# A fused attention and feed-forward kernel: a new order of steps from the eighth batch's kv sums on

## The chip, the cores and the metric

The kernel runs on one core of a Trainium2 chip. A core has five engines, each with its own queue of instructions that it takes strictly in order: PE (TensorE, matrix products), DVE (VectorE), ACT (ScalarE), POOL (GpSimd) and SP (SyncE, which here issues nearly all DMAs). Semaphores tie the queues together. The metric is the device time of one execution in microseconds (us); lower is better.

## The reference

It is an attention with cosine weights, whose output is the input of a two-layer feed-forward net.

```python
# q, k, v: (8, 8, 576, 64); c, s: cos and sin of pi/2 * position/576
def phi(x, c, s):
    r = np.maximum(x, 0.0)
    return np.concatenate([r * c, r * s], axis=-1)
q_p, k_p = phi(q, cos_w, sin_w), phi(k, cos_w, sin_w)
kv = np.einsum('bhsf,bhsd->bhfd', k_p, v)
z = np.sum(k_p, axis=2)
num = np.einsum('bhsf,bhfd->bhsd', q_p, kv)
den = np.einsum('bhsf,bhf->bhs', q_p, z)[..., None] + 1e-06
x = (num / den).transpose(0, 2, 1, 3).reshape(4608, 512)
...
h = x @ w_in                    # 512 x 2048
g = np.maximum(0.01 * h, h)
return g @ w_out                # 2048 x 512
```

## The kernel before

**The work.** There are nine groups of 512 tokens: groups 0 to 7 are the first 512 tokens of each batch, and group 8 collects the last 64 tokens of all eight batches. For a batch b, `k_cos(b,j,e)` and `k_sin(b,j,e)` make the weighted keys of token block j (tile kp, L428 on DVE and POOL, L426 on ACT), `v_pairs` casts the values (tile vm), and `kv_sum(b,...)` is the sum over tokens of keys times values: 72 small matmuls on PE (L503) and a cast by ACT to the tile kv (L510). `q_prep(g,j,...)` weights the queries (tile qp), `q_transpose_dma` turns them by DMA (tile qpT), `num(g,j)` multiplies them by kv on PE (L587), `den` and `rec` take the denominators, and `mul` writes x (tile xs). `x_transpose_dma(g)` turns that into the tile xT. `load_qtail(i)` loads the queries of two batches' tails for group 8 (tile qtl; two DMAs, L311) into a buffer that result tiles use as well: both have the tag osb, with four buffers.

**The feed-forward.** Each of the two large products is cut in halves of both operands and done with seven products of half the size in place of eight (the known scheme of Strassen, in a form with shared sums). `P(g,u,n)` is product n of the first layer for unit u of group g: four matmuls of 128x128 by 128x256 (L791). `x_sum(g,n,e)` makes the sums of xT's pieces that some of these products take. `e(g,u,x)` are the steps that read them out: b, s and S are copies (b on ACT, B on DVE; s on ACT, S on DVE), w and y are adds on DVE (L684), and a, c, d and e are the leaky relu on ACT, which write the tiles G. `g_sum` are sums of G's pieces on DVE. `F(g,i)` are products of the second layer, four matmuls each (L910), `R(g,n,e)` read their results out to the tiles osb, and `S(g,n)` stores a result (one DMA on SP, L1117).

For group 7, the eighth batch, each half-size product of the second layer is cut once more. Its operands' sums are the 28 steps `TS(n,k,e)` (`t_sum`, four sums of w_out's pieces for each of the products 1 to 7, tile tsum, 128x512 numbers in f16) and `AS(g,n,k,e)` (`a_sum`, the same for G's pieces, tile asum). `F2(g,n,j)` are the products (L1058), `R2` reads out, `C` combines. A helper, `tt_op`, records every sum of two tensors, so these all stand as L684.

**The order.** Nothing is scheduled when the kernel runs. A table PROGRAM lists all 1455 steps in the order in which they are recorded; each engine's queue is what is left of that list for it, and tiles and semaphores follow from it. The last letter of most steps names the engine: D for DVE, A for ACT, P for POOL. So a step that moves in the table may move on one engine, past what stands ahead of it there, and a changed letter takes the work to another queue.

```python
for name, args in parse(PROGRAM):
    OPS[name](*args)
```

The kv sums of the eighth batch, `kv_sum(7,0,4,n)`, stand in the table behind most of group 5's first layer and some of group 6's.

Of the kernel before, what the change touches and what calls it, by code (L numbers as in the profile page):

```python
# [107 lines left out]
e(5,1,e) k_sin(7,1,A) R(4,2,A) F(4,12) e(5,2,b) P(5,1,4) S(3,5) P(5,2,6) num(6,3) P(5,2,2) g_sum(4,3,5,8,2)  # L108
k_sin(7,0,D) e(5,1,d) e(5,2,a) e(5,1,c) e(5,2,w) q_prep(7,1,0,8,P) F(4,13) k_sin(7,5,P) den(6,3) load(v,7) S(3,3)
S(3,4) q_transpose_dma(7,0) F(4,14) P(5,2,3) P(5,3,1) F(4,15) P(5,2,7) P(5,3,5) F(4,16) rec(6,3) g_sum(4,4,0,4)  # L110
mul(6,3) e(5,2,e) e(5,2,y) e(5,3,b) x_transpose_dma(6) e(5,3,s) v_pairs(7,2,4,A) e(5,2,c) F(4,17) P(5,3,6) P(5,3,2)
k_cos(7,2,D) load_qtail(0) R(4,7,D) g_sum(4,4,4,8) e(5,3,w) F(4,20) F(4,18) P(5,2,4) F(4,21) F(4,19) R(4,5,D) P(5,3,7)
e(5,3,y) k_cos(7,0,D) q_prep(7,3,0,8,D) x_sum(6,1,D) k_cos(7,4,A) e(5,3,a) P(5,3,3) F(4,22) e(5,2,d) e(5,3,c)
x_sum(6,3,D) F(4,24) F(4,25) F(4,23) P(6,0,1) F(4,26) F(4,27) P(5,3,4) g_sum(5,1,4,8,2) x_sum(6,2,D) k_sin(7,8,P)
v_pairs(7,0,2,P) TS(1,1,P) k_sin(7,6,P) TS(6,1,P) k_cos(7,3,P) k_sin(7,7,P) e(5,3,e) e(6,0,b) P(6,0,5) e(5,3,d)
P(6,0,2) k_cos(7,1,D) P(6,0,6) P(6,1,1) e(6,0,a) e(6,0,s) k_cos(7,5,D) k_cos(7,6,D) k_sin(7,2,A) R(4,4,D) k_cos(7,7,D)
# [5 lines left out]
F(5,8) P(6,2,1) q_prep(8,2,0,8,P) den(7,1) q_prep(8,1,0,8,A) e(6,1,y) rec(7,1) mul(7,1) num(7,2) F(5,9) P(6,1,4)
e(6,1,e) R(5,6,D) TS(1,4,D) TS(5,1,D) e(6,2,s) e(6,2,b) e(6,1,d) TS(2,4,D) TS(1,3,D) S(4,3) S(4,2) load_qtail(3)
q_transpose_dma(8,0) P(6,2,6) F(5,10) P(6,3,1) F(5,11) e(6,2,w) R(5,2,A) den(7,2) P(6,2,3) F(5,12) F(5,16) num(7,3)
P(6,2,2) e(6,2,e) e(6,2,a) e(6,3,b) e(6,1,c) q_prep(8,3,0,8,A) g_sum(5,3,5,8,2) rec(7,2) TS(7,1,D) mul(7,2) den(7,3)
rec(7,3) F(5,13) P(6,2,7) P(6,3,5) F(5,14) P(6,3,2) F(5,15) F(5,17) num(8,0) P(6,3,6) F(5,18) mul(7,3) F(5,19)
R(5,7,D) e(6,2,y) e(6,3,s) e(6,2,c) e(6,3,a) TS(4,3,P) TS(6,2,P) TS(5,2,P) g_sum(5,4,4,8) g_sum(5,4,0,4)
x_transpose_dma(7) den(8,0) e(6,3,w) R(5,5,D) F(5,20) F(5,21) F(5,22) F(5,23) P(6,3,7) P(6,2,4) x_sum(7,1,P) TS(7,3,P)
e(6,3,y) R(5,4,D) P(6,3,3) F(5,24) x_sum(7,3,D) g_sum(6,1,0,4,1) g_sum(6,1,4,8,2) TS(4,1,D) e(6,2,d) e(6,3,c) P(6,3,4)
F(6,0) F(5,25) P(7,0,1) x_sum(7,2,D) e(6,3,e) e(6,3,d) e(7,0,b) g_sum(6,2,4,8,2) rec(8,0) mul(8,0) P(7,0,5) F(5,26)  # L130
P(7,0,6) F(6,1) g_sum(6,1,5,8,2) F(6,2) F(5,27) num(8,1) P(7,0,2) e(7,0,s) e(7,0,a) TS(6,4,D) e(7,0,w) F(6,3) P(7,0,3)
R(6,1,A) e(7,0,e) g_sum(6,2,0,4,1) R(5,3,D) den(8,1) x_sum(7,4,D) g_sum(6,2,5,8,2) P(7,0,7) F(6,4) P(7,1,1) P(7,1,5)
e(7,1,b) g_sum(6,3,5,8,2) e(7,0,y) g_sum(6,3,4,8,2) rec(8,1) e(7,1,S) e(7,0,c) q_transpose_dma(8,1) F(6,8) F(6,5)
F(6,6) P(7,1,6) F(6,9) num(8,2) F(6,7) mul(8,1) e(7,1,w) den(8,2) F(6,10) P(7,1,7) rec(8,2) TS(4,2,D) mul(8,2)
g_sum(6,3,0,4,1) R(6,6,D) P(7,0,4) P(7,1,2) F(6,11) P(7,1,3) F(6,12) num(8,3) e(7,1,y) e(7,1,a) TS(2,3,D)
g_sum(6,4,0,4) den(8,3) TS(7,2,D) TS(5,3,D) rec(8,3) mul(8,3) e(7,0,d) S(5,4) S(5,2) F(6,13) P(7,2,1) P(7,2,5)
R(6,2,A) e(7,1,e) e(7,2,b) e(7,2,s) e(7,1,c) P(7,1,4) F(6,16) P(7,2,6) F(6,17) F(6,14) P(7,2,2) TS(7,4,P) TS(5,4,P)
TS(6,3,D) x_transpose_dma(8) e(7,2,w) e(7,1,d) e(7,2,a) P(7,2,7) P(7,2,3) P(7,3,1) F(6,18) F(6,15) P(7,3,5) e(7,2,e)
g_sum(6,4,4,8) e(7,2,y) TS(4,4,D) TS(3,1,D) e(7,3,b) x_sum(8,1,P) e(7,2,c) e(7,3,s) P(7,3,6) g_sum(7,1,0,4,1) F(6,19)
P(7,2,4) e(7,3,w) R(6,7,D) P(7,3,2) e(7,2,d) x_sum(8,2,P) P(7,3,7) P(8,0,1) F(6,20) P(7,3,3) e(7,3,y) g_sum(7,3,0,4,1)  # L140
TS(3,3,D) S(5,3) S(5,5) g_sum(7,2,0,4,1) P(7,3,4) F(6,21) e(7,3,c) e(7,3,e) R(6,5,D) e(7,3,a) e(8,0,b) e(7,3,d)
F(6,22) F(6,23) P(8,0,5) AS(7,2,1,D) F2(7,1,1) x_sum(8,4,P) AS(7,1,1,D) AS(7,1,2,P) P(8,0,6) P(8,0,2) F2(7,1,2)
F(6,24) F(6,25) F(6,26) e(8,0,s) F2(7,1,4) R(6,4,D) x_sum(8,3,D) g_sum(7,1,4,8,2) AS(7,2,2,D) e(8,0,w) AS(7,1,3,D)
AS(7,2,3,D) AS(7,1,4,D) F(6,27) F2(7,1,5) P(8,0,7) F2(7,1,6) R(6,3,D) e(8,0,y) P(8,0,3) F2(7,1,7) g_sum(7,3,4,8,2)
F2(7,1,3) P(8,1,1) g_sum(7,1,5,8,2) AS(7,2,4,D) g_sum(7,2,4,8,2) TS(3,2,D) g_sum(7,2,5,8,2) TS(3,4,D) AS(7,6,1,D)
AS(7,5,1,D) e(8,0,a) R2(7,1,A) P(8,1,5) F2(7,6,1) AS(7,6,3,D) AS(7,6,2,D) S(6,5) S(6,2) S(6,3) P(8,0,4) F2(7,2,1)
F2(7,2,2) F2(7,2,4) AS(7,6,4,D) e(8,1,s) e(8,0,e) e(8,1,b) F2(7,2,5) F2(7,2,6) F2(7,2,7) F2(7,2,3) P(8,1,2) F2(7,6,2)
P(8,1,6) R2(7,2,A) C(7,2,1,P) e(8,1,w) e(8,1,a) e(8,0,c) F2(7,6,4) F2(7,6,5) g_sum(7,3,5,8,2) F2(7,6,7) F2(7,5,1)
F2(7,5,2) F2(7,6,6) F2(7,5,4) P(8,2,5) F2(7,6,3) P(8,1,3) P(8,1,7) C(7,2,2,D) AS(7,5,3,D) AS(7,7,1,D) g_sum(7,4,0,4)
e(8,1,y) e(8,0,d) R2(7,6,A) AS(7,5,2,P) AS(7,7,2,P) F2(7,7,1) P(8,2,1) F2(7,5,5) F2(7,7,2) e(8,1,e) e(8,2,b) e(8,2,S)  # L150
AS(7,7,3,D) AS(7,5,4,D) AS(7,7,4,D) e(8,1,c) F2(7,7,4) F2(7,7,5) P(8,2,2) F2(7,5,6) F2(7,7,6) P(8,1,4) F2(7,5,7)
g_sum(7,4,4,8) F2(7,5,3) F2(7,7,7) F2(7,7,3) P(8,2,6) AS(7,4,1,D) e(8,2,a) e(8,1,d) R2(7,7,A) AS(7,3,1,D) e(8,2,w)
AS(7,4,2,P) R2(7,5,D) C(7,5,1,P) C(7,5,2,P) AS(7,4,4,P) C(7,5,4,P) P(8,3,5) F2(7,4,1) F2(7,4,2) AS(7,4,3,D) F2(7,4,5)
P(8,2,7) P(8,2,3) P(8,3,1) F2(7,3,1) F2(7,4,4) F2(7,3,2) e(8,2,y) e(8,2,e) e(8,3,b) P(8,2,4) P(8,3,6) F2(7,3,4)
F2(7,4,7) F2(7,3,5) AS(7,3,3,D) AS(7,3,2,D) F2(7,3,6) F2(7,4,6) F2(7,3,7) F2(7,4,3) e(8,3,s) e(8,2,c) R2(7,4,A)
e(8,2,d) e(8,3,w) P(8,3,7) AS(7,3,4,D) g_sum(8,1,0,4,1) P(8,3,3) F2(7,3,3) P(8,3,2) e(8,3,y) P(8,3,4) e(8,3,e)
e(8,3,a) e(8,3,c) e(8,3,d) g_sum(8,1,4,8,2) R2(7,3,D) C(7,4,1,P) C(7,2,4,P) g_sum(8,1,5,8,2) g_sum(8,2,0,4,1)
g_sum(8,2,4,8,2) g_sum(8,3,4,8,2) g_sum(8,2,5,8,2) C(7,5,3,D) C(7,3,1,D) F(8,0) F(8,20) F(8,16) F(8,1) F(8,2) F(8,4)
F(8,3) R(8,1,A) F(8,5) F(8,6) F(8,8) F(8,7) F(8,9) C(7,2,3,P) C(7,4,2,D) g_sum(8,3,5,8,2) C(7,4,3,D) g_sum(8,3,0,4,1)
C(7,3,2,D) R(8,6,D) F(8,10) F(8,11) F(8,17) R(8,2,A) F(8,12) F(8,13) C(7,3,4,D) g_sum(8,4,0,8) C(7,3,3,D) F(8,14)  # L160
C(7,4,4,P) F(8,15) F(8,21) F(8,18) F(8,19) F(8,22) F(8,23) R(8,7,D) R(8,5,D,0) R(8,4,D) R(8,5,D,1) F(8,24) S(6,4)
# [1196 lines left out]
```

## Time and profile before

| | |
|---|---|
| Median of 3 runs | 271.87 us (271.45 to 272.15) |
| Profiled execution | 271.46 us |
| Its span, first to last instruction | 269.7 us |
| Mean granted PE clock | 0.997 |
| Instructions in the span | 7414 |
| DMA | 57.09 MB in 75041 packets |

The span is what the trace shows; 1.76 us of the execution lie around it. In the page an engine's line gives its busy time, the share of the span and the number of instructions. In a timeline a row is: start, length, engine, line, operation, output <- inputs, shape, and in brackets how long the engine had been idle and what ended that. Rows that follow each other alike are put in one, with their count after an x. The profile names tiles by name without a buffer's number. "SPq" is SP issuing a DMA; the DMA's own time from issue to landing is given apart.

### The profile page before, as it was taken

What the parts mean: (1) busy time and instruction counts of PE and PEld (TensorE: products, weight loads), DVE (VectorE), ACT (ScalarE), POOL (GpSimd) and SP (SyncE); (2) the same over time, 40 slices, a digit from 0 to 9 for tenths busy, and PEclk for the clock granted to TensorE, in tenths of its full rate; (3) what the DMA queues carried; (4) which work ended last, traced back from release to release, by engine and by line L of the source; (5) the groups of instructions that cost most, each with busy time, mean ns of one, the idle gap of its engine ahead of it and who ended that gap; (6) DMA issues with size and microseconds to landing.
All of it is one profiled execution on the core that took longest, in us unless ns stands there. A gap on an engine that the chain in (4) does not pass through costs nothing.

```text
span 269.7 us, 7414 instructions
## 1 busy us (share of the span) xinstructions
PE 261.9 (97%) x3009; PEld 222.9 (83%) x3009; DVE 225.1 (83%) x485; ACT 184.8 (69%) x333; POOL 111.3 (41%) x99
## 2 busy tenths in 40 slices
...
GB/s 232 359 396 413 379 400 371 389 243 238 255 242 337 116 237 231 324 238 259 233 265 191 155 393 147 156 157 121 117 158 79 2 79 79 106 52 2 41 115 158
DMA packets 75041, 57.09 MB, mean 212 GB/s; under 512 B 47232, under 2 KB 63616, under 8 KB 74624
## 3 DMA queue, kind: packets, MB, share of 16 engines
...
q14 instruction: 10, 0.08, 0.1%
...
## 4 chain that ended last, share of the span: by engine, by line
PE 86%; ACT 5%; DMA 3%; DVE 3%; issue 1%; SPq 1%; ACTq 0%; DVEq 0%
PE ps_f L791 31%; PE ps L910 26%; PE ps_h L634 10%; PE ps_o L658 5%; PE ps_kv L503 3%; DMA vst<-in_v_dram 3%; PE ps_num L587 2%; PE ps L1058 2%; ACT qp L426 2%; PE ps_y L1058 2%; PE ps_f L910 1%; ACT vm L434 1%; PE ps_xT L1207 1%; ACT G L823 1%; PE ps_kv L1158 1%
## 5 line engine op out<-in xcount | busy, mean ns | idle before, releaser
L823 ACT ACTIVATE G<-ps_f 128x512 f16<-128x512 f32 x84 | 48.7, 597 | 29.2 <-PE ps_f L791 26.4
L910 PE MATMUL ps<-w,G 128*128 128x256 f16 x432 | 59.6, 273 | 0.1
L910 PEld LDWEIGHTS <-G 128*128 128x128 f16 x560 | 53.7, 98 | 5.9 <-DVE G L684 0.4
L791 PE MATMUL ps_f<-xT,w 128*128 128x256 f16 x336 | 49.4, 273 | 0.1
L791 PEld LDWEIGHTS <-w 128*128 128x128 f16 x448 | 47.8, 113 | 1.1 <-issue 0.2
L791 PEld LDWEIGHTS <-wsum 128*128 128x128 f16 x336 | 36.2, 114 | 2.3 <-issue 1.0
L910 PE MATMUL ps<-T,ext 128*128 128x256 f16 x208 | 29.6, 273 | 0.0
L634 PE MATMUL ps_h<-xT,w 128*128 128x512 f16 (+1 forms) x144 | 29.1, 355 | 0.0
L428 POOL TENSOR_SCALAR kp<-kst,sin_t 128x256 f16<-128x256 f32 x17 | 22.7, 1341 | 11.2 <-PE ps_kv L503 6.2
L791 PE MATMUL ps_f<-X,wsum 128*128 128x256 f16 x176 | 26.0, 273 | 0.3 <-ACT s L434 0.3
L634 PEld LDWEIGHTS <-w 128*128 128x128 f16 x144 | 15.9, 114 | 10.9 <-POOL w L436 0.2
L910 PEld LDWEIGHTS <-ext 128*128 128x128 f16 x224 | 21.6, 98 | 2.2
L684 DVE TENSOR_TENSOR ps_f<-ps_f,s 128x512 f32<-128x512 f32 x28 | 19.4, 694 | 4.5 <-PE ps_f L791 2.4
L684 DVE TENSOR_TENSOR y<-ps_f,s 128x512 f32<-128x512 f32 x28 | 19.2, 684 | 3.6 <-PE ps_f L791 2.6
L645 ACT ACTIVATE G<-ps_h 128x1024 f16<-128x1024 f32 x16 | 15.9, 1022 | 7.2 <-PE ps_h L634 7.2
L611 DVE TENSOR_TENSOR xs<-ps_num,rden 128x512 f16<-128x512 f32 x28 | 19.3, 688 | 0.7
L823 ACT ACTIVATE G<-y 128x512 f16<-128x512 f32 x28 | 17.7, 632 | 2.6 <-DVE y L684 2.5
L428 POOL TENSOR_SCALAR qp<-qst,cos_t 128x512 f16<-128x512 f32 (+1 forms) x5 | 9.5, 1907 | 22.1 <-DMA qpT<-qp 17.8
L434 ACT COPY ps_f<-ps_f 128x512 f32<-128x512 f32 x27 | 15.6, 578 | 3.5 <-PE ps_f L791 3.1
L791 PE MATMUL ps_f<-xT,wsum 128*128 128x256 f16 x112 | 16.8, 273 | 0.8 <-DVE ps_f L684 0.8
L791 PE MATMUL ps_f<-X,w 128*128 128x256 f16 x112 | 16.8, 273 | 0.0
L684 DVE TENSOR_TENSOR osb<-ps,ext 128x512 f32<-128x512 f32 x20 | 13.6, 684 | 3.0 <-PE ps L910 2.8
...
## 6 DMA issues: line engine op xcount, KB each, us to landing
...
```

Source lines behind the costliest of these rows:

```text
L428: eng.tensor_scalar(out=o, in0=i, scalar1=0.0, scalar2=col, op0=ALU.max, op1=ALU.mult)
L434: nc.scalar.copy(o, i)
L503: nc.tensor.matmul(ps[:, o, (c - lo) * NE : (c - lo + 1) * NE], lhsT=st["kp", b][sl, c, j, :], rhs=vm[sl, c, j, :], start=(j == 0), stop=( ...
L611: nc.vector.tensor_tensor(out=xs(), in0=ps[:, :, 0 : 4 * NE].rearrange("p a (b e) -> p a b e", e=NE)[:, :, :, 0:D], in1=st["rden", *k].rea ...
L634: nc.tensor.matmul(ps[:, m % 2, lo:hi], lhsT=w1[m // 4, c][0][:, w1[m // 4, c][1], m % 4 : 512 : 4], rhs=xT[:, lo // P : hi // P, c, :], s ...
L645: nc.scalar.activation(st["g", g][:, m - 1 : m + 1, :], ps, AF.Lrelu)
L658: nc.tensor.matmul(st["ps_o", g, tt], lhsT=st["g", g][:, m, tt * P : (tt + 1) * P], rhs=w2[:, m, :], start=(m == 0), stop=(m == NFT - 1),)
L684: eng.tensor_tensor(out=o, in0=a, in1=b, op=op)
L791: nc.tensor.matmul(ps[:, mi * HT : (mi + 1) * HT], lhsT=a[:, c, 2 * r0 + mi : 512 : 4], rhs=b[:, c], start=(n in (1, 5) and mi == 0 and c ...
L823: nc.scalar.activation(st["g", g][:, m : m + 2, r * HT : (r + 1) * HT], {"a": A, "c": y22, "e": E, "d": B_}[e].rearrange("p (m t) -> p m t ...
L910: nc.tensor.matmul(ps[:, tt], lhsT=a[:, i, tt * P : (tt + 1) * P], rhs=b[:, i], start=(first and i == 4 * halves[0]), stop=(i == NPR - 1 a ...
L1058: nc.tensor.matmul(ps, lhsT=a[:, i], rhs=b[:, i], start=(fresh and i == 0), stop=(i == NI - 1), skip_group_check=True,)
```

## The change

The table PROGRAM gets a new order from its 833rd step to its end, and 39 steps another engine. The steps themselves are the same 1455, with the same sizes. In words: the steps ahead of the eighth batch's kv sums are placed as they would be if group 7 had no second cut, the kv sums themselves stand earlier among the products, and the sums TS, which the table had put partly in front of the kv sums, stand behind it, all but `TS(1,1,P)` and `TS(1,3,P)`; the steps behind have new places. The table has one line fewer, so line numbers of the functions are lower by one (L684 becomes L683).

```diff
-P(6,0,3) q_prep(8,0,0,8,A) F(5,3) e(6,0,e) e(6,1,b) kv_sum(7,0,4,n) S(4,5) g_sum(5,2,5,8,2) e(6,0,y)
...
+x_sum(6,3,D) R(4,4,D) e(6,0,s) e(6,0,w) R(4,3,D) g_sum(5,1,4,8,2) load_qtail(0) q_prep(8,0,0,8,A) kv_sum(7,0,4,n)
...
```

Steps that change the engine: `k_sin(7,1)`, `(7,3)` and `k_cos(7,4)` go from ACT to DVE, `k_sin(7,0)` and `k_cos(7,2)` from DVE to POOL, `q_prep(7,3)` and `k_cos(7,1)`, `(7,5)`, `(7,6)` and `(7,7)` from DVE to ACT, `k_sin(7,2)` and `q_prep(8,1)` from ACT to POOL, `q_prep(8,2)`, `k_sin(7,5)` and `(7,7)` from POOL to ACT, `e(5,3,s)` from ACT to DVE; `x_sum(6,4)`, `(7,2)` and `(8,3)` from DVE to POOL and `(8,1)`, `(8,2)`, `(8,4)` from POOL to DVE; of the sums TS five go from POOL to DVE and five the other way; three AS and four C change as well.

On DVE, from the sum g_sum(4,3,5,8,2) on (the first row; before, the second row is k_sin(7,0), and the add into ps_f is e(5,2,w)):

```order
L684 TENSOR_TENSOR G0_95<-G0_95 128x2x256
L428 TENSOR_SCALAR kp_2842<-kst_2838,sin_t_160 128x4x64
L684 TENSOR_TENSOR ps_f1_1378<-ps_f2_1379,s5_183 128x512
L597 TENSOR_SCALAR den_2907<-ps_num_2881 128x8
L603 RECIPROCAL rden_2944<-den_2907 128x8
```

And now:

```order
L683 TENSOR_TENSOR G0_95<-G0_95 128x2x256
L683 TENSOR_TENSOR ps_f1_1378<-ps_f2_1379,s5_183 128x512
L427 TENSOR_SCALAR kp_2842<-kst_2838,sin_t_160 128x4x64
L596 TENSOR_SCALAR den_2911<-ps_num_2897 128x8
L602 RECIPROCAL rden_2952<-den_2911 128x8
```

The add e(5,2,w) now follows the sum directly; the kp row behind it is k_sin(7,3), and k_sin(7,0) is on POOL.

On POOL beside it, from q_prep(7,1) (the two qp rows) to the last of the eighth batch's keys that POOL makes (vm is the cast v_pairs, tsum are sums of w_out's pieces), before:

```order
L428 TENSOR_SCALAR qp_2789<-qst_2420,cos_t_159 128x8x64
L428 TENSOR_SCALAR qp_2789<-qst_2420,sin_t_160 128x8x64
L428 TENSOR_SCALAR kp_2842<-kst_2838,sin_t_160 128x4x64 x2
L436 CAST vm_167<-vst_2909 128x18x64
L684 TENSOR_TENSOR tsum_3051<-w2_105 128x512
L428 TENSOR_SCALAR kp_2842<-kst_2838,sin_t_160 128x4x64
L684 TENSOR_TENSOR tsum_3054<-T2_178 128x512
L428 TENSOR_SCALAR kp_2842<-kst_2838,cos_t_159 128x4x64
L428 TENSOR_SCALAR kp_2842<-kst_2838,sin_t_160 128x4x64
```

And now, up to q_prep(8,1):

```order
L427 TENSOR_SCALAR qp_2789<-qst_2420,cos_t_159 128x8x64
L427 TENSOR_SCALAR qp_2789<-qst_2420,sin_t_160 128x8x64
L427 TENSOR_SCALAR kp_2842<-kst_2838,sin_t_160 128x4x64
L683 TENSOR_TENSOR tsum_2914<-w2_105 128x512
L427 TENSOR_SCALAR kp_2842<-kst_2838,sin_t_160 128x4x64
L427 TENSOR_SCALAR kp_2842<-kst_2838,cos_t_159 128x4x64
L435 CAST vm_167<-vst_2906 128x18x64
L683 TENSOR_TENSOR tsum_2914<-w2_105 128x512
L427 TENSOR_SCALAR kp_2842<-kst_2838,sin_t_160 128x4x64 x2
L427 TENSOR_SCALAR kp_2842<-kst_2838,cos_t_159 128x4x64
L427 TENSOR_SCALAR qp_3096<-qtl_2945,cos_t_159 128x8x64
L427 TENSOR_SCALAR qp_3096<-qtl_2945,sin_t_160 128x8x64
```

The cast moved behind one sum and two more key steps, and a pair of query steps on a tail tile stands behind the keys.

On SP, from the queries' transpose of group 7 (q_transpose_dma(7,0)) on, before:

```order
L540 DMA_TRANSPOSE qpT_2913<-qp_2789 128x16x128
L554 DMA_TRANSPOSE xT_2951<-xs_2766 128x16x128
L311 DMA qtl_2969<-in_q_dram 64x8x64 x2
L1117 DMA out_0_dram<-osb_2995 128x2x256
L540 DMA_TRANSPOSE qpT_3203<-qp_2773 128x16x128
L311 DMA qtl_3205<-in_q_dram 64x8x64 x2
```

And now (the first pair of tail loads is load_qtail(1), osb_2999 is S(4,5), and the second pair is load_qtail(0)):

```order
L539 DMA_TRANSPOSE qpT_2917<-qp_2789 128x16x128
L1116 DMA out_0_dram<-osb_2660 128x2x256
L1116 DMA out_0_dram<-osb_2677 128x2x256
L310 DMA qtl_2945<-in_q_dram 64x8x64 x2
L553 DMA_TRANSPOSE xT_2965<-xs_2766 128x16x128
L1116 DMA out_0_dram<-osb_2999 128x2x256
L1116 DMA out_0_dram<-osb_2864 128x2x256
L310 DMA qtl_3093<-in_q_dram 64x8x64 x2
L1116 DMA out_0_dram<-osb_3086 128x2x256
L539 DMA_TRANSPOSE qpT_3292<-qp_2773 128x16x128
```

load_qtail(0), ahead of all stores here before, now stands behind the stores S(4,5) and S(4,2).

More of the change, by code (lines that the diff above doesn't have):

```diff
@@ L107 @@
 load(k,7) den(6,2) k_cos(7,8,D) rec(6,2) R(4,6,D) e(5,1,y) e(5,2,S) mul(6,2) F(4,10) F(4,11) P(5,2,1) k_sin(7,4,A)
[L108 to L116, printed above, removed]
@@ L122 @@
[L122 to L131, printed above, removed]
@@ L132 @@
[L132 to L161, printed above, removed]
@@ L162 @@
-S(7,2) S(7,4) S(7,5) S(8,2) S(7,3) F(8,25) S(8,5,0) S(8,4) F(8,26) R(8,3,D,0) S(8,5,1) S(8,3,0) F(8,27) R(8,3,D,1)
-S(8,3,1)
+e(5,1,e) R(4,2,A) e(5,2,b) F(4,12) P(5,1,4) P(5,2,6) P(5,2,2) g_sum(4,3,5,8,2) e(5,1,d) e(5,1,c) e(5,2,a) e(5,2,w)
+F(4,16) F(4,13) num(6,3) load(v,7) k_sin(7,3,D) q_prep(7,1,0,8,P) den(6,3) k_sin(7,8,P) TS(1,1,P) S(3,5)
+q_transpose_dma(7,0) S(3,4) S(3,3) P(5,2,3) P(5,3,5) F(4,14) P(5,3,1) P(5,2,7) F(4,17) load_qtail(1) F(4,15) rec(6,3)
+k_sin(7,0,P) k_sin(7,7,A) e(5,2,e) mul(6,3) g_sum(4,4,0,4) e(5,2,y) e(5,3,b) k_cos(7,1,A) v_pairs(7,2,4,A) R(4,7,D)
@@ new lines @@
+k_cos(7,4,D) x_transpose_dma(6) F(4,18) P(5,2,4) P(5,3,6) F(4,19) F(4,20) F(4,21) P(5,3,2) e(5,3,S) q_prep(7,3,0,8,A)
+e(5,3,w) R(4,5,D) g_sum(4,4,4,8) k_cos(7,0,D) S(4,5) S(4,2) e(5,2,c) e(5,3,a) P(5,3,3) F(4,24) P(5,3,7) e(5,3,y)
+e(5,3,e) e(5,2,d) e(5,3,c) F(4,25) x_sum(6,1,D) k_sin(7,1,D) x_sum(6,2,D) g_sum(5,1,5,8,2) g_sum(5,1,0,4,1) F(4,26)
+F(4,27) P(5,3,4) F(4,22) F(4,23) P(6,0,1) k_cos(7,7,A) k_sin(7,5,A) e(5,3,d) k_cos(7,3,P) v_pairs(7,0,2,P) TS(1,3,P)
+k_sin(7,2,P) k_sin(7,6,P) k_cos(7,2,P) e(6,0,b) k_cos(7,6,A) k_cos(7,5,A) P(6,1,1) P(6,0,5) P(6,0,2) P(6,0,6) e(6,0,a)
@@ new lines @@
+x_sum(6,3,D) R(4,4,D) e(6,0,s) e(6,0,w) R(4,3,D) g_sum(5,1,4,8,2) load_qtail(0) q_prep(8,0,0,8,A) kv_sum(7,0,4,n)
+F(5,0) P(6,1,5) P(6,0,3) F(5,1) F(5,2) g_sum(5,2,5,8,2) P(6,0,7) TS(7,1,D) q_prep(8,1,0,8,P) g_sum(5,2,0,4,1) num(7,0)
+e(6,0,e) x_sum(6,4,P) e(6,1,b) g_sum(5,2,4,8,2) TS(2,1,D) den(7,0) F(5,4) F(5,3) g_sum(5,3,4,8,2) P(6,1,2) P(6,1,6)
+e(6,0,y) e(6,1,s) e(6,1,w) F(5,5) P(6,0,4) F(5,6) e(6,1,a) R(5,1,A) e(6,0,c) e(6,0,d) P(6,1,7) P(6,2,5) P(6,1,3)
+num(7,1) F(5,7) P(6,2,1) rec(7,0) g_sum(5,3,0,4,1) mul(7,0) S(4,4) q_transpose_dma(7,1) q_transpose_dma(8,0)
@@ new lines @@
+load_qtail(2) e(6,1,y) P(6,1,4) TS(2,2,D) den(7,1) e(6,1,e) F(5,8) e(6,2,s) e(6,2,b) e(6,1,d) TS(2,4,P)
+g_sum(5,3,5,8,2) rec(7,1) mul(7,1) R(5,6,D) P(6,2,6) e(6,2,w) num(7,2) F(5,9) F(5,12) F(5,10) P(6,2,3) num(7,3)
+F(5,13) P(6,2,2) P(6,2,7) F(5,11) P(6,3,1) F(5,14) den(7,2) e(6,1,c) e(6,2,e) e(6,2,a) R(5,2,A) rec(7,2) mul(7,2)
+F(5,15) F(5,16) e(6,3,b) den(7,3) TS(4,3,P) F(5,17) P(6,3,5) P(6,3,6) F(5,18) F(5,19) rec(7,3) mul(7,3) TS(6,1,D)
+TS(5,1,P) x_transpose_dma(7) S(4,3) e(6,2,y) TS(1,2,D) q_prep(8,2,0,8,A) R(5,7,D) g_sum(5,4,4,8) TS(6,2,D) TS(5,2,D)
```

40 lines of the change are left out of this document (36 added, 4 removed).

## The prediction

> **What bounds the kernel now.** I read the page's busy times first, then each engine's busy time by stretch, then the timeline of PE for gaps between products, and last the chain of waits and the timelines of DVE and POOL at those gaps.
>
> ```profile
> PE 261.9 (97%) x3009; PEld 222.9 (83%) x3009; DVE 225.1 (83%) x485; ACT 184.8 (69%) x333; POOL 111.3 (41%) x99
> ```
>
> TensorE is busy for 97% of the 269.7 us. The next view gives five stretches; the columns are the stretch, its length, then PE, weight loads, DVE, ACT and POOL busy with their counts, the granted clock and the DMA share.
>
> ```profile
> 161.60:183.00 21.40, 20.44 (x252) 18.84 (x250) 18.38 (x38) 14.26 (x27) 7.71 (x7) 1.00 0.67 149
> 183.00:207.00 24.00, 23.65 (x258) 21.68 (x258) 20.05 (x47) 15.13 (x28) 11.37 (x8) 1.00 0.66 132
> 207.00:229.00 22.00, 22.00 (x239) 20.55 (x234) 18.93 (x41) 12.76 (x24) 6.17 (x5) 1.00 0.20 50
> 229.00:253.00 24.00, 23.88 (x315) 23.40 (x314) 23.50 (x49) 15.10 (x29) 10.22 (x11) 1.00 0.13 45
> 253.00:262.00 9.00, 9.00 (x85) 8.10 (x83) 8.38 (x19) 3.02 (x6) 3.25 (x4) 1.00 0.28 93
> ```
>
> The clock is full, so only PE's gaps can be won. The table's first changed step stands at about 162 us. Behind it PE waits at three places. In its timeline (start, length, line, operation, count) a product's four matmuls show 0.60, but products start 0.44 apart, as 163.57 to 164.01 shows.
>
> ```profile
> 163.57 0.60 PE L791 MATMUL ps_f<-xT,w 128*128 128x256 f16 x4
> 164.01 1.34 PE L910 MATMUL ps<-w,G 128*128 128x256 f16 x8
> 166.18 0.60 PE L791 MATMUL ps_f<-xT,wsum 128*128 128x256 f16 x4 [0.83 <-DVE ps_f L684]
> ...
> 204.01 0.60 PE L910 MATMUL ps<-w,G 128*128 128x256 f16 x4
> 204.95 0.63 PE L791 MATMUL ps_f<-X,wsum 128*128 128x256 f16 x4 [0.35 <-ACT s L434]
> ...
> 232.44 0.39 PE L1058 MATMUL ps<-tsum,asum 128*128 128x128 f16 x4
> 232.96 0.60 PE L791 MATMUL ps_f<-xT,w 128*128 128x256 f16 x4
> ```
>
> First place: eight matmuls from 164.01 should let the next product start at 164.01 + 0.88 = 164.89; it starts at 166.18, so 1.29 is lost. Second: 204.01 + 0.44 = 204.45 against 204.95, 0.50 lost. Third: four half-width matmuls take half a product, 232.44 + 0.22 = 232.66 against 232.96, 0.30 lost. Together 2.09. DVE and POOL show the cause.
>
> ```profile
> 163.05 1.31 DVE L684 TENSOR_TENSOR G<-G 128x512 f16<-128x512 f16 x1
> 164.28 1.24 DVE L428 TENSOR_SCALAR kp<-kst,sin_t 128x256 f16<-128x256 f32 x1
> 165.44 0.69 DVE L684 TENSOR_TENSOR ps_f<-ps_f,s 128x512 f32<-128x512 f32 x1
> ...
> 188.72 0.42 DVE L684 TENSOR_TENSOR tsum<-w,tsum 128x512 f16<-128x512 f16 x1
> ...
> 189.72 0.42 DVE L684 TENSOR_TENSOR tsum<-w 128x512 f16<-128x512 f16 x1
> ...
> 201.98 1.31 DVE L684 TENSOR_TENSOR xT<-xT 128x512 f16<-128x512 f16 x1
> 204.49 0.41 DVE L684 TENSOR_TENSOR X<-xT,X1b 128x512 f16<-128x512 f16 x1
> 230.57 1.05 DVE L684 TENSOR_TENSOR xT<-xT 128x512 f16<-128x512 f16 x1
> ```
> ```profile
> 157.89 2.00 POOL L428 TENSOR_SCALAR qp<-qst,sin_t 128x512 f16<-128x512 f32 x1
> 159.86 2.32 POOL L428 TENSOR_SCALAR kp<-kst,sin_t 128x256 f16<-128x256 f32 x2
> 162.93 1.15 POOL L436 CAST vm<-vst 128x1152 f16<-128x1152 f32 x1 [0.74 <-DMA vst<-in_v_dram]
> 164.04 1.33 POOL L684 TENSOR_TENSOR tsum<-w 128x512 f16<-128x512 f16 x1
> ...
> 187.70 1.99 POOL L428 TENSOR_SCALAR qp<-qtl,cos_t 128x512 f16<-128x512 f32 x1
> 189.68 2.25 POOL L428 TENSOR_SCALAR qp<-qtl,sin_t 128x512 f16<-128x512 f32 x1
> ...
> 201.86 1.15 POOL L684 TENSOR_TENSOR tsum<-w 128x512 f16<-128x512 f16 x1
> 230.19 1.15 POOL L684 TENSOR_TENSOR asum<-asum,G 128x512 f16<-128x512 f16 x1 [1.08 <-ACT s L434]
> ```
>
> A 512-wide f16 sum takes DVE 0.42 (188.72). At 163.05 it takes 1.31, beside POOL's cast; at 164.28 a quarter-width prep ends only after POOL's sum of w_out's pieces; 201.98 and 230.57 lie beside a POOL sum too. So a POOL sum or cast costs a simultaneous DVE operation up to 1.31 - 0.42 = 0.89, and here PE pays. Beside POOL's TENSOR_SCALAR (187.70 to 191.9) DVE's sums keep their 0.42.
>
> [...]
>
> **The change part by part.** *PE.* The same products, so the same PE work; nothing is added. The eighth batch's kv sums pass seven products, 7 x 0.44 = 3.1. *First place.* F(4,16) moves ahead of F(4,13), and g_sum(4,3,5,8,2) no longer meets the cast: POOL's queue is now the prep that ends at 159.89, one kp prep (1.16) to 161.05, a sum to 162.20, two kp preps to 164.52, and only then the cast of v. k_sin(7,0) has left DVE, so e(5,2,w) follows at 163.5 instead of 165.44. I take the whole 1.29 as saved; the ends are 0 and 1.29. *Second place.* x_sum(7,2) goes from DVE to POOL and no sum of w_out stands on POOL beside x_sum(7,3): 0.50 saved, ends 0 and 0.50. *Third.* x_sum(8,3) goes to POOL and (8,1), (8,2), (8,4) to DVE, and a_sum(7,1,2) no longer meets it: 0.30, ends 0 and 0.30.
>
> *Engines.* ACT gains six kp preps (0.46 each, 178.69 below) and two pairs of q preps (two halves of 0.72, 179.50 below), and loses four, one pair and a copy of 0.6: about +1.8 net, covered by its 21.40 - 14.26 = 7.1 idle in the first stretch. DVE loses six kp preps and one q prep and gains three preps and a copy. Of the 28 sums five go each way between DVE and POOL. Two, TS(1,1) and TS(1,3), still stand ahead of the kv sums. The freed DVE time is worth nothing by itself.
>
> *SP.* Here the order changes most, and waits go past other issues.
>
> ```profile
> 159.91 4.21 SPq L540 DMA_TRANSPOSE qpT<-qp  x1
> 167.62 1.32 SPq L554 DMA_TRANSPOSE xT<-xs  x1
> 169.03 1.98 SPq L311 DMA_DIRECT2D qtl<-in_q_dram  x2
> ...
> 178.69 0.91 ACT L426 ACTIVATE kp<-kst,sin_t 128x256 f16<-128x256 f32 x2
> 179.50 0.72 ACT L426 ACTIVATE qp<-qtl,cos_t 128x512 f16<-128x512 f32 x1
> 181.56 1.32 PE L503 MATMUL ps_kv<-vm,kp 64*128 64x66 f16 x72
> 182.91 0.60 ACT L510 CAST kv<-ps_kv 128x528 f16<-128x528 f32 x1 [0.49 <-PE ps_kv L503]
> ```
>
> load_qtail(0) went out at 169.03. It now takes the osb buffer of S(4,5), behind R(4,5), which by the queues ends at about 170.9. The store's landing and the pair's are bounded by two rows, min, median and max from issue to landing, of the tile osb from 150 to 190 us and of qtl:
>
> ```profile
> DMA to landing us min/median/max: 2.1/4.4/9.3
> DMA to landing us min/median/max: 2.7/3.3/4.5
> ```
>
> Two issues took 1.98, the second starting some 1.1 after the first, so a pair is in place 3.8 to 5.6 after its first issue. That puts the tail in place at 170.9 + 2.1 + 3.8 = 176.8 at best, at 180.9 with 4.4 and 5.6, at 185.8 at worst. q_prep(8,0) stands on ACT ahead of the kv cast, e(6,0,e) and e(6,1,b). The kv sums move from 181.56 to 181.56 - 1.29 - 3.06 = 177.2; they take some 1.2, and six products follow before num(7,0), at about 181.0. Ahead of that ACT needs two halves of 0.72 and a cast of 0.60, 2.0 together: the tail costs nothing until about 179. Little else is in flight then, as for the pair at 169.03, so I take 178, cost 0; both ends stay for the range.
>
> *Give-back.* By the queues, kv_sum(7) has 0.2 of margin behind ACT's k_cos(7,5), P(6,0,2) 0.1, P(6,1,7) 0.2, num(7,1) 0.2, P(6,2,6) 0.05, num(8,2) and F2(7,2,1) 0.15. A few of these break by some tenths, or POOL meets DVE once at a place that counts. Between 0 and the whole 2.09 I take 0.5, near the second place's loss. No gain beyond 2.09 is left in this part of the program, since PE waits nowhere else.
>
> The sum: the profiled execution is 271.46 (span 269.7 and 1.76 around it). 271.46 - 2.09 + 0.5 = 269.87. The median of the runs is 271.87, 0.41 above, so 270.3. I use 0.3%, 0.82 us, as what a measurement tells from no change.
>
> **Rivals.** *A. The tail load is late (slower).* If S(4,5) lands late, q_prep(8,0) holds ACT, num(7,0) and P(6,1,2) wait, one for one beyond 179. Landing at 180.9 costs 1.9 and cancels the gain: 271.7. From 182 on it is slower by over 0.82; at 185.8 it costs 6.8: 271.87 - 2.09 + 6.8 = 276.6. Against it: the queue is short after 170. Chance 0.08.
>
> *B. x_transpose(7) lands late (no change).* x_sum(7,1) and (7,2) now follow each other on POOL, at 1.15 a sum, instead of running on both engines, so by the queues a landing beyond 199 makes PE wait at F(6,0), one for one. Before (start, then the landing of xT from 193 to 202):
>
> ```profile
> 194.38 1.91 SPq L554 DMA_TRANSPOSE xT<-xs  x1
> DMA to landing us min/median/max: 6.2/6.2/6.2
> ```
>
> that was 200.6. In the new order it is due out at about 191.5, so landed by 197.7; if it slips by 2.7 it costs 1.4: 271.87 - 2.09 + 1.4 = 271.2. Chance 0.06.
>
> *C. DVE becomes the bound (no change, or slower).* In the stretch from 229 on DVE is busy 23.50 of 24.00. The time won ahead of it arrives there as PE waiting on DVE: each further meeting of a POOL sum costs 0.89 against 0.50 of idle. Three meetings: 3 x 0.89 - 0.50 = 2.17, no change (271.9); four, 3.06, slower (272.8). POOL has as many sums there after as before, which speaks against it. Chance of no change 0.12, of slower 0.12.
>
> *D. Every POOL operation holds DVE, preps too (no change).* q_prep(8,1), now on POOL for some 4 us around 170.3, would then stop g_sum(4,4,4,8) and k_cos(7,0), and e(5,3,y) behind them: a 2.0 half less a 0.42 sum is about 1.5, so 271.87 - 2.09 + 1.5 = 271.3. [...] Against it: the 0.42 at 188.72. Chance 0.05.
>
> *E. The places don't close*, because a new wait stands right behind at the same hand-off: 271.5 to 272.2. Chance 0.07.
>
> **How the numbers follow.** The forecast's case has the remaining 0.50 and its own range 269.5 (less than 0.3 given back, by the runs' spread of 0.35 either way) to 271.0. Same: B 0.06, C 0.12, D 0.05, E 0.07, together 0.30. Slower: A 0.08, C 0.12, together 0.20. For eight in ten the range goes from 269.4 to 272.9, which leaves out the worse half and more of the slower cases and little below.
>
> **What would show it.** Right: no gap over 0.2 on PE between 162 and 168; g_sum(4,3,5,8,2) at 0.42; kv sums on PE at about 177.1; no wait of the row after x_sum(7,2). Wrong: ACT waiting on a DMA into qtl at 177 to 183 (A); POOL waiting on xT near 199 (B); PE rows with releaser DVE from 229 to 253 (C); DVE sums longer than 0.42 beside a POOL TENSOR_SCALAR (D).

## The result, and the profile after

The changed kernel takes 269.98 us (median of 6 runs, 269.58 to 270.79) against 271.74 for the kernel before in the same comparison: a ratio of 0.9941, 95% interval 0.9923 to 0.9959. That is 1.76 us faster. The forecast was 270.3, and faster. The profiled execution takes 269.58 with a span of 267.7.

The page's busy times, and the table by stretch (same columns and stretches as for the kernel before):

```profile
PE 261.3 (98%) x3009; PEld 222.9 (83%) x3009; DVE 224.2 (84%) x480; ACT 185.8 (69%) x336; POOL 113.2 (42%) x101
```
```profile
161.60:183.00 21.40, 21.40 (x269) 20.18 (x268) 18.45 (x37) 16.68 (x32) 14.38 (x11) 1.00 0.74 161
183.00:207.00 24.00, 24.00 (x262) 22.18 (x261) 20.45 (x45) 14.90 (x29) 8.63 (x7) 1.00 0.53 116
207.00:229.00 22.00, 22.00 (x231) 20.54 (x229) 20.22 (x43) 12.70 (x24) 5.19 (x5) 1.00 0.26 67
229.00:253.00 24.00, 24.00 (x314) 23.55 (x313) 23.04 (x49) 16.01 (x30) 10.83 (x10) 1.00 0.04 13
253.00:262.00 9.00, 9.00 (x85) 8.06 (x83) 7.74 (x17) 1.17 (x2) 2.62 (x3) 1.00 0.62 204
```

PE is now busy for the whole of every stretch. In PE's timeline the three places read, first place, second, third:

```profile
164.01 0.60 PE L909 MATMUL ps<-w,G 128*128 128x256 f16 x4
164.45 0.42 PE L586 MATMUL ps_num<-kv,qpT 128*128 128x66 f16 x8
164.71 0.60 PE L790 MATMUL ps_f<-xT,wsum 128*128 128x256 f16 x4
...
202.56 1.04 PE L909 MATMUL ps<-w,G 128*128 128x256 f16 x8
203.44 0.60 PE L790 MATMUL ps_f<-X,wsum 128*128 128x256 f16 x4
...
230.45 0.61 PE L1057 MATMUL ps<-tsum,asum 128*128 128x128 f16 x8
230.89 0.60 PE L790 MATMUL ps_f<-xT,w 128*128 128x256 f16 x4
```

Every row starts where the one before it lets it: 202.56 + 2 x 0.44 = 203.44, and 230.45 + 0.44 = 230.89. The brackets that named a wait are gone. The rows by which I compare kernels are the start of P(5,0,1), ahead of the changed part, and the start of the last product, F(8,27). For P(5,0,1), before and after:

```profile
146.80 0.63 PE L791 MATMUL ps_f<-xT,w 128*128 128x256 f16 x4
```
```profile
146.62 0.63 PE L790 MATMUL ps_f<-xT,w 128*128 128x256 f16 x4
```

F(8,27) is the last four matmuls of these rows, two matmuls (0.22) after their start, before and after:

```profile
265.06 0.82 PE L910 MATMUL ps_f<-w,G 128*128 128x256 f16 x6
```
```profile
262.77 0.82 PE L909 MATMUL ps_f<-w,G 128*128 128x256 f16 x6
```

The stretch between those two starts took 118.47 before and takes 116.37 now: 2.10 less. The start was 0.18 earlier, the end of the span comes 0.28 later behind PE's last product, and 0.12 more lies around the span: 2.10 + 0.18 - 0.28 - 0.12 = 1.88 = 271.46 - 269.58. Nothing ahead of P(5,0,1) was changed, and its start lay between 146.5 and 147.9 in the kernels that follow. So the stretch is a sharper measure than the time, and each verdict below rests on it and on PE's rows first; but it is one execution of each kernel, where a median has up to twelve. Where a table has another number of lines, the same function's line number is one higher or lower.

The experiments ran on three chips, each time beside the kernel before. Its medians there were 271.50 (for POOL order, sums behind, late places and three places), 271.05 (seven moves, collision put back, one block, late tail) and 271.53 (the three rows "again" and the DVE dose). A ratio is taken within its comparison and need not be the quotient of the two medians.

| kernel | stretch on PE | median | ratio to before (95%) |
|---|---|---|---|
| before | 118.47 | 271.74 | |
| changed | 116.37 | 269.98 | 0.9941 (0.9923 to 0.9959) |
| changed, again | 116.38 | 270.37 | 0.9963 (0.9945 to 0.9980) |
| POOL order only | 117.09 | 270.50 | 0.9964 (0.9942 to 0.9987) |
| sums behind only | 117.56 | 270.90 | 0.9972 (0.9951 to 0.9992) |
| late places only | 116.74 | 270.21 | 0.9957 (0.9930 to 0.9984) |
| three places, six moves | 117.26 | 270.00 | 0.9938 (0.9918 to 0.9958) |
| seven moves | 116.51 | 270.04 | 0.9967 (0.9940 to 0.9995) |
| seven moves, again | 116.88 | 270.01 | 0.9956 (0.9938 to 0.9975) |
| collision put back | 117.56 | 271.04 | 0.9993 (0.9973 to 1.0013) |
| one block | 116.38 | 270.94 | 0.9996 (0.9975 to 1.0017) |
| one block, again | 116.43 | 270.32 | 0.9964 (0.9944 to 0.9984) |
| late tail | 125.34 | 278.53 | 1.0268 (1.0222 to 1.0314) |
| DVE dose | 117.01 | 270.51 | 0.9991 (0.9972 to 1.0010) |

### The profile page after: what moved, and what is told of

Its sections match the earlier page's. It is cut to its first block, busy times and chain, and to the rows that moved or that the text cites. A ratio compares the mean times of both kernels' runs of the same rounds, so it can differ in the third digit from the quotient of the medians.

```text
span 267.7 us, 7405 instructions
## 1 busy us (share of the span) xinstructions
PE 261.3 (98%) x3009; PEld 222.9 (83%) x3009; DVE 224.2 (84%) x480; ACT 185.8 (69%) x336; POOL 113.2 (42%) x101
## 4 chain that ended last, share of the span: by engine, by line
PE 89%; ACT 4%; DMA 4%; DVE 1%; SPq 1%; issue 0%; DVEq 0%; ACTq 0%
PE ps_f L790 32%; PE ps L909 28%; PE ps_h L633 10%; PE ps_o L657 5%; PE ps_kv L502 3%; DMA vst<-in_v_dram 3%; PE ps_num L586 3%; PE ps L1057 2%; ACT qp L425 2%; PE ps_y L1057 2%; DMA out_dram<-osb 1%; ACT vm L433 1%; PE ps_xT L1206 1%; PE ps_kv L1157 1%; PE ps_numh L1192 1%; PE ps_qt L575 1%
## 5 line engine op out<-in xcount | busy, mean ns | idle before, releaser
L427 POOL TENSOR_SCALAR kp<-kst,sin_t 128x256 f16<-128x256 f32 x17 | 21.4, 1264 | 10.8 <-PE ps_kv L502 6.1
L683 DVE TENSOR_TENSOR ps_f<-ps_f,s 128x512 f32<-128x512 f32 x28 | 19.5, 695 | 5.4 <-ACT s L433 2.8
L683 DVE TENSOR_TENSOR y<-ps_f,s 128x512 f32<-128x512 f32 x28 | 19.2, 684 | 1.9 <-PE ps_f L790 1.4
L683 DVE TENSOR_TENSOR osb<-ps,ext 128x512 f32<-128x512 f32 x20 | 13.5, 681 | 2.5 <-PE ps L909 2.3
```

The source lines that it names most:

```text
L427: eng.tensor_scalar(out=o, in0=i, scalar1=0.0, scalar2=col, op0=ALU.max, op1=ALU.mult)
L683: eng.tensor_tensor(out=o, in0=a, in1=b, op=op)
```

## The experiments

Theory T: PE waited at three places for a DVE operation that a POOL sum or cast held up, and the gain is those waits. Theory R: the place of the kv sums, and the sums ahead of them, carry it.

**POOL order only**, on the kernel before (POOL's steps alone are shown):

```diff
-k_sin(7,8,P) v_pairs(7,0,2,P) TS(1,1,P) k_sin(7,6,P) TS(6,1,P) k_cos(7,3,P) k_sin(7,7,P)
+k_sin(7,8,P) k_sin(7,6,P) k_cos(7,3,P) k_sin(7,7,P) v_pairs(7,0,2,P) TS(1,1,P) TS(6,1,P)
```

> The kernel before, with one edit on POOL: the cast v_pairs(7,0,2) and the sums TS(1,1) and TS(6,1) stand behind the key preps k_sin(7,6), k_cos(7,3) and k_sin(7,7) instead of ahead of or among them. Theory T (at each of three places PE waits for a DVE operation that a POOL sum or cast held up): g_sum(4,3,5,8,2) falls from 1.31 to about 0.42 us, the PE gap before P(5,2,3) closes, and the time falls by 1.29, to about 270.4. Theory R (it is the place of the kv sums, and the w_out sums ahead of them, that count): no change, 271.7, since the kv sums and the sums still stand where they stood.

DVE's rows at the first place in this kernel, and the product that had waited there:

```profile
163.50 0.41 DVE L684 TENSOR_TENSOR G<-G 128x512 f16<-128x512 f16 x1
163.83 0.57 DVE L428 TENSOR_SCALAR kp<-kst,sin_t 128x256 f16<-128x256 f32 x1
...
165.36 0.60 PE L791 MATMUL ps_f<-xT,wsum 128*128 128x256 f16 x4
```

The sum fell from 1.31 to 0.41, and the gap closed (the eight matmuls ahead of it start at 164.48, and 164.48 + 0.88 = 165.36); the stretch is 1.38 shorter than before, with the kv sums where they were. T holds and R falls for this place.

**Sums behind only**: on the kernel before, the part for which the change is named.

```diff
-v_pairs(7,0,2,P) TS(1,1,P) k_sin(7,6,P) TS(6,1,P) k_cos(7,3,P) k_sin(7,7,P) ... TS(1,2,D) ... kv_sum(7,0,4,n)
+v_pairs(7,0,2,P) k_sin(7,6,P) k_cos(7,3,P) k_sin(7,7,P) ... kv_sum(7,0,4,n) TS(1,1,P) TS(6,1,P) TS(1,2,D)
```

> The kernel before, with only the part that the change is named for: TS(1,1), TS(6,1) and TS(1,2) moved behind the eighth batch's kv sums. Theory T: the cast still holds g_sum(4,3,5,8,2) to about 1.31, but k_sin(7,0) behind it finds a key prep on POOL in place of a sum and takes 0.35 instead of 1.24; P(5,2,3) then starts at about 165.3 instead of 166.18, so the time falls by about 0.85, to 270.9. Theory R: the whole first part of the gain, about 1.3, to 270.4. If it is only the cast that counts: no change.

```profile
163.60 0.41 DVE L684 TENSOR_TENSOR G<-G 128x512 f16<-128x512 f16 x1
163.94 1.23 DVE L428 TENSOR_SCALAR kp<-kst,sin_t 128x256 f16<-128x256 f32 x1
...
163.75 1.27 POOL L436 CAST vm<-vst 128x1152 f16<-128x1152 f32 x1 [1.01 <-DMA vst<-in_v_dram]
```

The stretch is 0.91 shorter, as T had it (0.85), but by another road: v landed later, the sum started 0.15 ahead of the cast and took 0.41, and the cast held k_sin(7,0) instead. One block was left instead of two. So the agreement in size does not show that moving the sums did it; the next run bears on that.

**Late places only**, on the kernel before: x_sum(7,3) away from a POOL sum, and two DVE steps behind e(8,0,w).

```diff
-x_sum(7,1,P) TS(7,3,P) ... TS(7,4,P)
+x_sum(7,1,P) ... TS(7,4,P) TS(7,3,P)
-x_sum(8,3,D) g_sum(7,1,4,8,2) AS(7,2,2,D) e(8,0,w)
+x_sum(8,3,D) e(8,0,w) g_sum(7,1,4,8,2) AS(7,2,2,D)
```

> The kernel before, with the second and third place alone: TS(7,3) on POOL moved behind TS(7,4), away from x_sum(7,3); and g_sum(7,1,4,8,2) and AS(7,2,2) on DVE moved behind e(8,0,w). Theory T: the gaps before P(7,0,6) (0.50) and P(8,0,7) (0.30) close, the time falls by 0.80, to about 270.9. If a freed gap is taken up by the next hand-off: between 271.3 and 271.7.

PE's two products now start where the ones before them let them (204.09 + 0.44 and 232.00 + 0.22):

```profile
204.53 0.60 PE L791 MATMUL ps_f<-X,wsum 128*128 128x256 f16 x4
...
232.22 0.60 PE L791 MATMUL ps_f<-xT,w 128*128 128x256 f16 x4
```

Both gaps closed, the third although x_sum(8,3) was still held (1.05): e(8,0,w) no longer had to wait for the two steps between them. But the stretch fell by 1.73, not 0.80: the first place, which was not touched, lost only 0.23 in this execution.

```profile
164.04 0.42 DVE L684 TENSOR_TENSOR G<-G 128x512 f16<-128x512 f16 x1
164.37 1.24 DVE L428 TENSOR_SCALAR kp<-kst,sin_t 128x256 f16<-128x256 f32 x1
...
164.23 1.22 POOL L436 CAST vm<-vst 128x1152 f16<-128x1152 f32 x1 [0.25 <-DMA vst<-in_v_dram]
```

Again the sum came first, by 0.19. In the kernel before, the cast had come first, by 0.12 (162.93 and 163.05). So 1.29 is what this place cost in one execution, and not a constant price.

**Three places, six moves**: both edits together (six steps moved, not the eight that the expectation counts).

> The kernel before, with the edits of both: eight steps moved, none to another engine, the kv sums where they were. Theory T: all 2.09 of PE's waiting goes, the time is that of the changed kernel, 269.7 to 270.0, and the other several hundred moves and 39 changes of engine are worth nothing. Theory R: well short of that, 270.9 or more.

The ratio equals that of the changed kernel (0.9938 against 0.9941). In the trace, though, a new gap of 0.76 stands at 169.92:

```profile
167.85 1.42 DVE L428 TENSOR_SCALAR kp<-kst,cos_t 128x256 f16<-128x256 f32 x1
169.19 0.68 DVE L684 TENSOR_TENSOR ext<-ps,ext 128x512 f32<-128x512 f32 x1
...
166.85 1.14 POOL L436 CAST vm<-vst 128x1152 f16<-128x1152 f32 x1
167.96 1.16 POOL L684 TENSOR_TENSOR tsum<-w 128x512 f16<-128x512 f16 x1
...
169.92 0.60 PE L910 MATMUL ps<-ext,G 128*128 128x256 f16 x4 [0.60 <-DVE ext L684]
```

The cast and the sum, pushed back, now hold k_cos(7,2), and the result R(4,7) behind it is late. With the first edit alone POOL ran 0.85 earlier and the same prep took 0.43. In the changed kernel k_cos(7,2) is on POOL, so that meeting cannot occur there. That this change of engine is what guards against it is argued: no run here makes it alone.

**Seven moves**: on the kernel before, the three sums behind the kv sums, the cast behind one more key prep, and the late places.

```diff
-v_pairs(7,0,2,P) TS(1,1,P) k_sin(7,6,P) TS(6,1,P) k_cos(7,3,P) k_sin(7,7,P)
+k_sin(7,6,P) v_pairs(7,0,2,P) k_cos(7,3,P) k_sin(7,7,P) ... kv_sum(7,0,4,n) TS(1,1,P) TS(6,1,P) TS(1,2,D)
```

> The kernel before, with seven steps moved and no engine changed: TS(1,1), TS(6,1) and TS(1,2) behind the kv sums, the cast v_pairs(7,0,2) behind one more key prep (k_sin(7,6)), and the later two places mended (TS(7,3) behind TS(7,4); g_sum(7,1,4,8,2) and AS(7,2,2) behind e(8,0,w)). Theory T: the cast now runs from about 164.7, where DVE waits for PE anyway, no POOL sum is left at k_cos(7,2), all three gaps close as in the changed kernel and none opens at 170; from P(5,0,1) to F(8,27) PE needs 116.4, as in the changed kernel, and the time is 269.7 to 270.0. Theory R (the many other moves carry part of the gain): 117 or more, 270.5 or more.

The same kernel once more, and the changed kernel beside it on one chip:

> The kernel before with seven steps moved, beside the changed kernel on the same chip. Theory T: equal to the changed kernel within the interval, 116.5 from P(5,0,1) to F(8,27). Theory R: slower than the changed kernel by 0.5 or more.

> The changed kernel itself, unedited, as the measure for the others on this chip. Every theory: from P(5,0,1) to F(8,27) 116.4, ratio to before near 0.994.

The first time the stretch was 116.51, with no gap, and the median 270.04. The second time, on one chip beside the changed kernel, medians were 270.01 for this and 270.37 for the changed kernel (ratios 0.9956 and 0.9963, intervals that overlap nearly whole). The trace of that second run has one gap of 0.39 before P(5,2,3) (stretch 116.88). I put it down to the cast meeting k_sin(7,0) again; no row of that trace is printed here. So seven moves without a change of engine give what the several hundred gave, within what the time can tell, but by that reading they leave one race (an outcome that hangs on which of two engines starts first) that neither of the changed kernel's two traces shows.

**Collision put back**, on the changed kernel, with PE's order left as changed:

```diff
-g_sum(4,3,5,8,2) ... TS(1,1,P) ... k_sin(7,0,P) ... k_cos(7,3,P) v_pairs(7,0,2,P) TS(1,3,P)
+g_sum(4,3,5,8,2) k_sin(7,0,D) ... TS(1,1,P) TS(1,3,P) v_pairs(7,0,2,P) ... k_cos(7,3,P)
```

> The changed kernel, with the collision put back at the first place and PE's order left as changed: k_sin(7,0) on DVE directly behind g_sum(4,3,5,8,2), and on POOL the sum TS(1,3) and the cast directly behind TS(1,1). Theory T: g_sum(4,3,5,8,2) and k_sin(7,0) are held one after the other, e(5,2,w) starts at about 165.0 instead of 163.4, P(5,2,3) at 165.7 instead of 164.71, and the time rises by 0.7 to 1.0, to about 270.9. If it was the order of F(4,16) and F(4,13) on PE that closed the gap: no change, 270.0.

```profile
162.61 1.37 DVE L683 TENSOR_TENSOR G<-G 128x512 f16<-128x512 f16 x1
163.90 1.23 DVE L427 TENSOR_SCALAR kp<-kst,sin_t 128x256 f16<-128x256 f32 x1
165.05 0.69 DVE L683 TENSOR_TENSOR ps_f<-ps_f,s 128x512 f32<-128x512 f32 x1
...
165.79 0.60 PE L790 MATMUL ps_f<-xT,wsum 128*128 128x256 f16 x4 [1.00 <-DVE ps_f L683]
```

The two blocks are back (1.37 and 1.23), the gap is back, and the stretch is 1.19 longer than in the changed kernel. The order of F(4,16) and F(4,13), left as changed, did not close it. In time the median is that of the kernel before beside it (271.04 and 271.05).

**One block**: the same, but k_sin(7,0) stays on POOL.

> As the kernel with the collision put back, but with k_sin(7,0) on POOL as in the changed kernel: g_sum(4,3,5,8,2) alone is held, to about 163.9. Theory T with slack: e(5,2,w) still ends by 164.6, ahead of P(5,2,3) at 164.71, no PE gap, 270.0. If each held DVE sum costs PE what it costs DVE: 0.5 to 0.9 more, 270.5 to 270.9.

> The kernel in which g_sum(4,3,5,8,2) alone may be held, once more: its trace had no PE gap (116.38), but its median was 270.94. Theory T with slack: the time is that of the changed kernel on this chip, within 0.3, and the higher median was the chip. If the profiled execution was a lucky one (the sum held by 0.14 only): 0.5 to 0.9 above the changed kernel, and a PE gap before P(5,2,3) in this trace.

No gap in either trace. The first median, 270.94, does not tell one block from two, which took 271.04 on the same chip; only the traces do (116.38 and 117.56). Beside the changed kernel on another chip one block took 270.32 against 270.37. In the first trace the sum was held by 0.14 only (0.55), so that a full block of g_sum alone costs nothing is not shown here.

**Late tail**: rival A, on the changed kernel.

```diff
-load_qtail(0) q_prep(8,0,0,8,A) kv_sum(7,0,4,n)
+S(4,4) q_transpose_dma(7,1) load_qtail(0) q_prep(8,0,0,8,A) kv_sum(7,0,4,n)
```

> The changed kernel, with load_qtail(0) issued behind S(4,4) and q_transpose_dma(7,1) on SP, so that the tail lands at 183.5 to 184.5 instead of 177.2. Rival A of the prediction: ACT stands at q_prep(8,0) until then, num(7,0) and P(6,1,2) wait, one for one beyond 179, so 4.5 to 5.5 more: 274.5 to 275.5. If ACT's idle time or other work takes most of it: under 2 more, below 272.

ACT's row, then PE's at num(7,0), then stretches of this kernel (the last three columns are granted clock, DMA share, GB/s):

```profile
184.84 0.72 ACT L425 ACTIVATE qp<-qtl,cos_t 128x512 f16<-128x512 f32 x1 [7.08 <-DMA qtl<-in_q_dram]
...
186.71 0.60 PE L586 MATMUL ps_num<-kv,qpT 128*128 128x66 f16 x8 [5.67 <-ACT kv L509]
...
185.00:187.00 2.00, 0.29 (x6) 0.29 (x6) 0.00 (x0) 2.00 (x4) 0.00 (x0) 0.56 0.01 4
187.00:191.00 4.00, 4.00 (x25) 2.88 (x23) 1.27 (x4) 2.41 (x6) 0.00 (x0) 0.50 0.00 0
191.00:193.00 2.00, 2.00 (x15) 1.64 (x14) 1.79 (x4) 1.11 (x2) 0.00 (x0) 0.74 0.03 8
193.00:197.00 4.00, 3.68 (x44) 3.35 (x43) 3.64 (x7) 2.69 (x5) 2.61 (x3) 1.00 0.36 69
```

The tail was used at 184.84, 5.8 after 179, and PE waited 5.7: that fits the threshold and the one-for-one wait. The whole cost is 8.97 of the stretch, above the 4.5 to 5.5 expected. The wait is 5.7 of it; PE was granted half its clock from the gap until about 192, which is, as an estimate from the granted clocks (mainly 4 us at 0.50 and 2 at 0.74), some 2.6 more, and smaller waits follow.

**DVE dose**: rival C, on the changed kernel.

```diff
-x_sum(8,4,D)
+x_sum(8,4,D) Z() Z() Z()     # each: tt_op(zt, b12, b11, ALU.subtract, DVE), zt read by nothing
```

> The changed kernel with three more sums of 128x512 f16 on DVE behind x_sum(8,4), at about 233, into a tile of their own: 3 x 0.34 = 1.0 us more on DVE. Rival C of the prediction, that DVE bounds the stretch from 229 to 253: PE loses most of that, about 0.9, with its gap between 233 and 243, time 270.7 to 271. If PE has the slack: no gap over 0.2, time as the changed kernel.

```profile
233.57 1.34 DVE L683 TENSOR_TENSOR zt<-w 128x512 f16<-128x512 f16 x3
...
239.26 0.60 PE L790 MATMUL ps_f<-xT,w 128*128 128x256 f16 x4 [0.21 <-DVE ps_f L683]
```

DVE's next step came 1.25 later (234.82 for 233.57), PE lost 0.21 and 0.39 near 239, and the stretch is 0.63 longer than 116.38: half of the dose. In the changed kernel the add into ps_f for which the product waits ends at 237.30 and the product starts at 237.97, so 0.67 of the 1.25 was free there. The time alone is unclear: the medians on one chip are 270.51 and 270.37, the ratios 0.9991 and 0.9963. So DVE has about 0.6 to give ahead of this product, and for this dose PE paid what went beyond.

## Why the prediction was right, point by point

*The places and their sum.* Right. PE's gaps of 1.29, 0.50 and 0.30 are gone, and the stretch fell by 2.10 against 2.09.

*The give-back.* The term of 0.5 was too large: the trace shows none. The thin margins, 0.05 to 0.2 by the queues, all held. With 0 in its place the sum is 271.46 - 2.09 = 269.37 for an execution that took 269.58. The medians are another matter: the gain was 1.76 in the first comparison and 271.53 - 270.37 = 1.16 in the second, against the 1.59 forecast. So that 270.3 came near is in part luck: a give-back that did not occur stood against a first place taken at its full price for every execution.

*First place.* Right in mechanism and in order. DVE's and POOL's rows after:

```profile
162.90 0.41 DVE L683 TENSOR_TENSOR G<-G 128x512 f16<-128x512 f16 x1
163.40 0.70 DVE L683 TENSOR_TENSOR ps_f<-ps_f,s 128x512 f32<-128x512 f32 x1
...
163.15 1.18 POOL L427 TENSOR_SCALAR kp<-kst,cos_t 128x256 f16<-128x256 f32 x1
164.28 1.19 POOL L435 CAST vm<-vst 128x1152 f16<-128x1152 f32 x1
```

The sum takes 0.41 again, e(5,2,w) starts at 163.40 (163.5 was worked out), the cast at 164.28 (164.52), and the kv sums start on PE at 177.03 (177.1). What the prediction did not see is that the 1.29 depends on when v lands: the trace with only the late places mended has the same steps there, but the cast started 0.19 behind the sum, and it lost 0.23. The median gains of 1.76 and 1.16 rather than 2.10 fit that. So does the spread of the kernel before: where the changed kernel ran again, the 35 executions of the kernel before took 270.11 to 272.72, eleven of them 270.63 or less, which lies within the changed kernel's 269.89 to 271.01. That those eleven escaped the wait is argued, since no trace shows one of them.

*Second place.* Right in result, wrong in a step. I wrote that no sum of w_out's pieces stands beside x_sum(7,3). One does:

```profile
197.22 1.48 POOL L683 TENSOR_TENSOR X<-xT,X1b 128x512 f16<-128x512 f16 x1
198.67 1.15 POOL L683 TENSOR_TENSOR tsum<-w,tsum 128x512 f16<-128x512 f16 x1
...
198.88 1.22 DVE L683 TENSOR_TENSOR xT<-xT 128x512 f16<-128x512 f16 x1
```

x_sum(7,3) is held as before (1.22), but x_sum(7,2), for which PE had waited behind it, was done on POOL by 198.7 (the first row), nearly 5 ahead of P(7,0,6). The gap closed by slack, not by taking the block away. In the kernel before the bracket at P(7,0,6) names ACT, but x_sum(7,2) on DVE ended at 204.90, just ahead of the product at 204.95, and with POOL's sum moved away (late places only) the gap was gone.

*Third place.* Right. x_sum(8,3) ran on POOL at 223.64, and e(8,0,w) ended on DVE at 229.88, 1.0 ahead of P(8,0,7) at 230.89.

Holds as such did not go away. From 162 us on, four DVE sums of 128x512 in f16 took over 1.2 in the changed kernel (1.38, 1.22, 1.38 and 1.39, against 0.41 alone) and two in the kernel before. PE waited at none of the four: what counts is whether a product is due behind the sum that is held.

*Rival A* did not occur: the tail was loaded at 173.28 and in place 3.9 later, at 177.2 (178 was taken). ACT took it at 177.69. Its price was too small: in the late tail PE's wait was one for one beyond 179 (5.7 for 5.8), but the cost, with the clock down to 0.50, was not (8.97 for that wait).

*Rival B* did not occur: xT, issued at 191.65, landed 4.3 later.

```profile
191.65 1.72 SPq L553 DMA_TRANSPOSE xT<-xs  x1
DMA to landing us min/median/max: 4.3/4.3/4.3
```

*Rival C*: DVE's busy time there fell from 23.50 to 23.04, and the dose shows the slack at one product there, 0.6.

*Rival D* is refuted. q_prep(8,1) ran on POOL as two preps, and DVE's sums beside them kept their time:

```profile
172.35 1.99 POOL L427 TENSOR_SCALAR qp<-qtl,sin_t 128x512 f16<-128x512 f32 x1
...
173.01 0.41 DVE L683 TENSOR_TENSOR X<-xT 128x512 f16<-128x512 f16 x1
173.61 0.42 DVE L683 TENSOR_TENSOR X<-xT,X 128x512 f16<-128x512 f16 x1
```

If every POOL operation held DVE, they would have been held; a POOL TENSOR_SCALAR did not hold them here (0.41 and 0.42 beside 1.99). Beside a smaller prep of 128x256 a DVE sum took up to 0.61 (at 65.44, ahead of the changed part), a slowing and not a hold.

*Rival E* did not occur: no gap stands behind any of the three places.

*What the change is named for.* Moving the sums alone gave a ratio of 0.9972, but its trace still lost 0.42 at the first place, where the untouched steps lost 0.23 with a similar landing of v. What it is worth by itself is left open. The earlier kv sums bought nothing that a run here shows: with them where they were, PE's gaps closed and the time was reached.
